# New instruction orders and PSUM banks for a polysketch attention with a gated feed-forward, and batch 1's loads held by a small copy

## The chip, the core and the metric

The kernel runs on one core of one Trainium2 chip. A core has five engines with instruction queues of their own: PE (TensorE, matrix products into PSUM), DVE (VectorE), ACT (ScalarE), POOL (GpSimd) and SP (SyncE, which issues DMA transfers). They run side by side and meet only at semaphores. PSUM has eight banks. The metric is the device time of one execution in microseconds (us); less is better. The median of three runs before the change is 101.96 us.

## The reference

```python
def phi(x):                       # S1, S2: 8 x 32; x: [4 batches, 4 heads, 1088, 32]
    a = np.einsum('rd,bhsd->bhsr', S1, x)
    b = np.einsum('rd,bhsd->bhsr', S2, x)
    return np.einsum('bhsi,bhsj->bhsij', a, b).reshape(*x.shape[:-1], r * r)
q_p, k_p = (phi(q), phi(k))
kv = np.einsum('bhsf,bhsd->bhfd', k_p, v)
z = np.sum(k_p, axis=2)
num = np.einsum('bhsf,bhfd->bhsd', q_p, kv)
den = np.einsum('bhsf,bhf->bhs', q_p, z)[..., None] + 1e-06
attn = num / den
x = attn.transpose(0, 2, 1, 3).reshape(4352, 128)
gate = np.maximum(x @ w_gate, 0.0)        # w_gate, w_val: 128 x 1536
val = x @ w_val
out = gate * val @ w_out                  # w_out: 1536 x 128, out: 4352 x 128
```

This is linear attention with 64 features for each row, and then a feed-forward with a rectified gate over the 4352 rows that it gives.

## The kernel before

The program is written as a list of 857 operations (`P.add(engine, name, function, after, ...)`), each for one engine. A table of numbers, `START`, gives each operation its place; operations are issued in the order of these numbers, so every engine's queue is a part of that one order, and each engine works through its queue in order. `after` and `RINGS` name predecessors for the search that made the table; at run time only true conflicts over data make an engine wait. A second table, `BANKS`, gives each piece of PSUM that is taken (a `Lease`) its bank or pair of banks, and a bank that is taken again waits for the reader that gives it up. Batch 0's first half has a path of its own (`class First`), for an early start; the other queries go through `class Q`, the keys of each batch through `class K`, the feed-forward through `class F`.

- Keys of a batch: load k, two DVE transposes to kT (`kt1`), PE products with the sketches (`ksk`), a DVE transpose back to kab (`kt2`), feature products kp on POOL (`kphi`; some of batch 0 on DVE), then `kv` on PE against v (cast to 16 bits by ACT, `vc`), and `kve` on DVE, which writes bd. The sum z goes PE, DVE (`zc`), PE (`w`), DVE (`wc`) into the query weights wq.
- Queries: load q, DVE transposes to qT (`qt1`), PE products with wq (`qsk`), DVE transposes to qabc (`qt2`), a denominator (`bw`, `red`, `rd`), features qqp on POOL (`qphi`), a transpose on SP's queue or PE (`qtr`), the numerator on PE (`num`), and a copy to xT. In `First` the names are fab, fqp, fpt, frT, and DVE writes xT (`xd`).
- Feed-forward: the rows are cut into groups, and each group into units of 512 columns of gate and value. 102 units each have a gate product `g` and a value product `v` on PE (0.22 us each), `relu` on ACT, a product `h` on DVE out of PSUM (for 19 units ACT copies the value and POOL multiplies, `hp`), and then an output block `o` of four matmuls, accumulated in PSUM over the units of a group. w_gate, w_val and w_out are used in thirds 0, 1, 2. Third 0 comes by SP and is cast by ACT (`cw`); thirds 1 and 2 (wg1, wv1, wg2, wv2, wo1, wo2) are loaded and cast by POOL's own transfers (L310).

Ahead of the named matmuls in `WARM`, PE is given matmuls of zeros into bank 7 (L1015), 55 in all. `gate` (L391) is a memset by POOL of one element of batch 1's k buffer: the load of k for batch 1 overwrites it, and so waits until POOL has come so far; the loads of q and v that follow stand behind it on SP's queue.

Of the kernel before, what the change touches and what calls it, by code (L numbers as in the profile page):

```python
# [10 lines left out]
FP16 = mybir.dt.float16  # L11
# [17 lines left out]
RINGS = [['ld s1', 'ld s2', 'ld k01', 'ld v000', 'ld v001', 'ld v002', 'ld v003', 'ld v010', 'ld v011', 'ld v012', 'ld v013'], ['mz', 'kt1 0 0'], ['fills', 'kt1 0 0'], ['zero', 'fills'], ['ld k00', 'ld q00', 'table'], ['zero', 'mz'], ['zero', 'sel'], ['id32', 'masks', 's1r'], ['kphi 0 8', 'ld wv1', 'ld wg2', 'ld wg1', 'ld wv2', 'gate', 'ld wo1', 'ld wo2'], ['ld v013', 'ld wg0', 'ld wv0', 'ld q01']]  # L29
# [71 lines left out]
]  # L101
WARM = {34: 29, 63: 2, 143: 14, 147: 1, 152: 9}


class Lease:
# [36 lines left out]
def kernel(  # L142
# [12 lines left out]
    nc = tc.nc  # L155
# [26 lines left out]
    def sb(shape, dt, name):  # L182
        return const.tile(shape, dt, name=name)

    P = Plan()
# [867 lines left out]
```

## Time and profile before

| | us |
|---|---|
| runs | 101.83, 101.96, 102.0 |
| span of the profiled execution | 100.1 |
| median of the runs less that span | 1.9 |
| PE busy | 94.2 |
| DVE busy | 82.7 |
| ACT busy | 84.1 |
| POOL busy | 65.8 |
| first feed-forward matmul starts | 14.58 |
| last matmul ends | 96.6 |

The execution's own time beyond its span is not listed, so the span is set beside the median of the runs. Rows of a timeline read: start, duration, engine, line of the kernel, operation, output and inputs, sizes, count, and in brackets how long the engine had been idle and what ended that. A matmul's duration includes its way through the array, so consecutive ones overlap. Rows of the chain read: start, duration, what the program's end hung on then. Buffers of one name are numbered in the program and unnumbered in the profile.

### The profile page before, as it was taken

Reading aid. Unit: us, or ns where it says so; the run is one execution under the profiler, and the core shown is the slowest. Engines: PE = TensorE matmul, PEld = TensorE weight load, DVE = VectorE, ACT = ScalarE, POOL = GpSimd, SP = SyncE. Lnnn points to the kernel's source line nnn. Section 1 sums busy time; section 2 is a strip of 40 time slices with the busy share of each in tenths; the row PEclk is TensorE's granted clock in tenths of the full one; section 3 lists DMA queues with packets and bytes.
Section 4 is the critical chain, followed back from the end, with each engine's and each line's share of the span. In section 5 each row is a group of like instructions: output and inputs, shape, how many; then the busy total and the mean of one; then the engine's idle time right before and its main releaser. Section 6 shows DMA issues by size and latency. Waiting matters only on the chain.

```text
span 100.1 us, 3180 instructions
## 1 busy us (share of the span) xinstructions
PE 94.2 (94%) x1223; PEld 68.3 (68%) x1223; DVE 82.7 (83%) x175; ACT 84.1 (84%) x169; POOL 65.8 (66%) x89
## 2 busy tenths in 40 slices
PE   6999989989999999999999999999999999999950
PEld 6978969848779965557673656765676665688940
DVE  4778779999989998999998689799746879897940
ACT  3445889999799798998999999899999999998730
POOL 6029947898988999999897699935944404001700
PEclk9999999999999999999999999999999999999999
DMA  2988889999930525208664200071217305003331
GB/s 43 370 229 267 146 122 358 339 269 276 342 125 0 111 66 134 45 12 235 165 182 99 60 0 7 1 169 27 52 29 120 78 0 129 2 7 84 99 105 52
DMA packets 14799, 12.40 MB, mean 124 GB/s; under 512 B 8256, under 2 KB 12352, under 8 KB 14784
## 3 DMA queue, kind: packets, MB, share of 16 engines
q1 hardware_dynamic: 13392, 10.70, 38.5%
q0 software_dynamic: 864, 0.79, 5.8%
q10 hardware_dynamic: 528, 0.72, 2.2%
q8 instruction: 9, 0.15, 0.7%
q14 instruction: 6, 0.05, 0.2%
HBM read 9.05 MB, written 2.23 MB: 113 GB/s over the span
## 4 chain that ended last, share of the span: by engine, by line
PE 81%; ACT 6%; POOL 4%; DMA 3%; issue 1%; DVE 1%
PE ps L916 42%; PE ps L944 23%; PE ps L1015 5%; ACT g_sb L921 4%; DMA wg<-in_moe_w_gate_dram 3%; PE ps L848 3%; PE ps L501 2%; PE ps L780 2%; POOL kp L543 2%; PE ps L567 2%; ACT v_sb L925 1%; POOL fqp L695 1%; ACT qpt L840 1%; PE ps L515 1%; POOL wv L310 1%
## 5 line engine op out<-in xcount | busy, mean ns | idle before, releaser
L921 ACT ACTIVATE g_sb<-ps 128x512 f16<-128x512 f32 x102 | 56.3, 613 | 3.9 <-PE ps L916 3.2
L931 DVE TENSOR_TENSOR ht<-g_sb,ps 128x512 f16<-128x512 f16 (+1 forms) x84 | 53.5, 673 | 7.2 <-PE ps L916 5.6
L916 PE MATMUL ps<-xT,wv 128*128 128x512 f16 (+1 forms) x132 | 35.6, 332 | 0.5 <-ACT g_sb L921 0.5
L916 PE MATMUL ps<-xT,wg 128*128 128x512 f16 (+1 forms) x132 | 34.3, 332 | 0.3 <-DMA wg<-in_moe_w_gate_dram 0.3
L944 PEld LDWEIGHTS <-ht 128*128 128x128 f16 x408 | 28.0, 98 | 9.2 <-issue 0.8
L944 PE MATMUL ps<-wo,ht 128*128 128x128 f16 x408 | 33.8, 219 | 0.0
L936 POOL TENSOR_TENSOR ht<-g_sb,v_sb 128x512 f16<-128x512 f16 x19 | 21.7, 1158 | 16.4 <-ACT g_sb L921 14.9
L916 PEld LDWEIGHTS <-wg 128*128 128x128 f16 x132 | 13.6, 115 | 5.9 <-issue 2.2
L543 POOL TENSOR_TENSOR kp<-kab 128x512 f16<-128x512 f32 (+2 forms) x14 | 15.7, 1136 | 2.0 <-DVE kab L507 2.0
L916 PEld LDWEIGHTS <-wv 128*128 128x128 f16 x132 | 13.9, 114 | 3.6 <-issue 1.3
L821 POOL TENSOR_TENSOR qqp<-qan,qabc 128x1024 f16<-128x1024 f32 (+1 forms) x9 | 14.9, 1658 | 0.4
L925 ACT CAST v_sb<-ps 128x512 f16<-128x512 f32 x19 | 11.3, 601 | 0.6 <-PE ps L916 0.5
L1015 PE MATMUL ps<-zero 128*128 128x128 f16 x55 | 5.9, 285 | 1.0 <-DVE zero L292 1.0
L793 DVE STREAM_TRANSPOSE qabc<-ps 128x128 f32<-128x128 f32 (+1 forms) x12 | 5.4, 488 | 1.0 <-PE ps L780 0.6
L987 DVE STREAM_TRANSPOSE qT<-q_sb 128x544 f32<-128x544 f32 (+2 forms) x9 | 5.9, 662 | 0.4 <-DMA q_sb<-in_q_dram 0.4
L1015 PEld LDWEIGHTS <-zero 128*128 128x128 f16 x55 | 5.1, 136 | 1.3 <-DVE zero L292 1.0
L951 ACT ACTIVATE o_sb<-ps 128x512 f32<-128x512 f32 (+1 forms) x10 | 5.2, 521 | 0.7 <-PE ps L944 0.7
L801 POOL TENSOR_TENSOR bw<-qabc 128x128 f32<-128x128 f32 (+1 forms) x9 | 3.7, 412 | 2.9 <-DVE qabc L793 2.9
L815 POOL TENSOR_TENSOR qan<-qabc,qrd 128x128 f32<-128x128 f32 (+1 forms) x9 | 3.3, 372 | 3.3 <-DVE qrd L811 3.3
L861 ACT CAST xT<-ps 128x512 f16<-128x512 f32 (+1 forms) x9 | 4.7, 517 | 0.5 <-PE ps L848 0.5
L491 DVE STREAM_TRANSPOSE kT<-k_sb 128x544 f32<-128x544 f32 x6 | 4.2, 724 | 0.0
L507 DVE STREAM_TRANSPOSE kab<-ps 128x576 f32<-128x576 f32 (+2 forms) x5 | 3.3, 664 | 0.7 <-PE ps L501 0.7
(94 smaller groups left out, 77.4 us busy)
## 6 DMA issues: line engine op xcount, KB each, us to landing
k_sb<-in_k_dram SPq DMA_DIRECT2D x3, 544.0 KB, 6.1
q_sb<-in_q_dram SPq DMA_DIRECT2D x3, 544.0 KB, 4.9
out_dram<-o_sb SPq DMA_DIRECT2D x22, 64.0 KB, 1.7
v<-in_v_dram SPq DMA_DIRECT2D x6, 144.0 KB, 7.7
v<-in_v_dram SPq DMA_DIRECT2D x6, 128.0 KB, 7.6
out_dram<-o_sb SPq DMA_DIRECT2D x16, 32.0 KB, 1.8
v<-in_v_dram SPq DMA_DIRECT2D x6, 64.0 KB, 3.1
k_sb<-in_k_dram SPq DMA_DIRECT2D x1, 288.0 KB, 3.5
```

The lines of the kernel that those rows point to most:

```text
L543: eng.tensor_tensor(out=self.kp[:, lo:hi].rearrange("p x g (i a c) -> p (x g i) a c", i=2, a=R), in0=a[:, :, :, None].to_broadcast([128, n ...
L793: nc.vector.transpose(self.abc[:, lo:lo + m, 2 * i2:2 * i2 + 2].rearrange("p x h f -> p h x f"), pair(ls[i2])[:, :, lo * 32:(lo + m) * 32] ...
L821: nc.gpsimd.tensor_tensor(out=self.qp[:, lo:hi].rearrange("p x g (i a c) -> p (x g i) a c", i=2, a=R), in0=self.an[:, lo * H:hi * H, :, No ...
L916: nc.tensor.matmul(bank(l)[:, y * self.W:(y + 1) * self.W], w[:, j // 4, :, j % 4], x, start=True, stop=True, skip_group_check=True)
L921: nc.scalar.activation(out=self.gs, in_=bank(l), func=ACTF.Relu)
L925: nc.scalar.copy(out=self.vs, in_=bank(l))
L931: nc.vector.tensor_tensor(out=self.ht[:, t], in0=self.gs[:, t], in1=bank(l)[:, t], op=ALU.mult)
L936: nc.gpsimd.tensor_tensor(out=self.ht, in0=self.gs, in1=self.vs, op=ALU.mult)
L944: nc.tensor.matmul(o[:, s], self.ht[:, i * 128:(i + 1) * 128], wo[:, j // 4, j % 4], start=(j == 0 and s == 0), stop=(j == NJ - 1), skip_g ...
L951: nc.scalar.mul(out=self.os[:, 0:n * DM], in_=bank(self.lo)[:, 0:n * DM], mul=1.0 / (XSCALE * XSCALE))
L987: nc.vector.transpose(qT[b][:, lo:hi], q_sb[b][:, lo:hi])
L1015: nc.tensor.matmul(PS[:, 7, 0:128], zero, zero, start=True, stop=True, skip_group_check=True)
```

## The change

Four things change. All of `START` and all of `BANKS` are replaced (each pair of banks is now one of neighbours, as it mostly was). In `RINGS` POOL's loads of weights have the order wg1, wv1, wg2, wv2, wo1, wo2, and no longer stand behind a key product. `WARM` loses 13 of the 55 zero matmuls. And `gate` is now a DMA that SP issues: it copies 16 bytes of the landed third 2 of w_gate into a new buffer, so that SP waits until that third has landed, and with SP everything behind it on its queue.

```diff
-RINGS = [..., ['kphi 0 8', 'ld wv1', 'ld wg2', 'ld wg1', 'ld wv2', 'gate', 'ld wo1', 'ld wo2'], ['ld v013', 'ld wg0', 'ld wv0', 'ld q01']]
+RINGS = [..., ['ld wg1', 'ld wv1', 'ld wg2', 'ld wv2', 'ld wo1', 'ld wo2'], ['ld v013', 'ld wg0', 'ld wv0', 'ld q01']]
 START = [
-    2, 5, 0, 8, 4, 42, 10, 11, 12, 16, 18, 23, 25, 29, 3, 13, 1, 14, 33, 68, 36, 87, 20, 98, 71,
+    2, 6, 1, 8, 5, 40, 9, 10, 12, 13, 15, 23, 26, 29, 3, 17, 0, 19, 33, 80, 37, 93, 20, 58, 65, 79,
...
 BANKS = [
-    (0,), (2,), (3, 4), (5, 6), (1,), (5,), (3,), (7,), (6, 7), (5,), (2,), (6,), (5, 6), (6,),
+    (0,), (0,), (1,2), (6,7), (3,), (1,), (7,), (6,), (3,4), (3,), (7,), (5,), (1,2), (7,), (6,),
...
-WARM = {34: 29, 63: 2, 143: 14, 147: 1, 152: 9}
+WARM = {34: 29, 143: 13}
...
-    g_op = P.add("POOL", "gate", lambda: nc.gpsimd.memset(k_sb[1][0:1, 0:1], 0.0))
+    gone = sb([1, 8], FP16, "gone")
+    g_op = P.add("SP", "gate", lambda: nc.sync.dma_start(
+        out=gone, in_=wg[0:1, 2, 0:2].rearrange("m p j -> m (p j)")), [lwl["g2"][1]])
```

Line numbers after the change are 3 to 5 less: L916 becomes L913, L310 becomes L305, L491 becomes L488.

On POOL, at the end of the start-up (s1r, feature products of batch 0's keys into kp and queries into fqp, weight loads by `DMA`), the queue before is:

```order
L379 TENSOR_TENSOR s1r<-wq,maskh 128x128
L543 TENSOR_TENSOR kp_93<-kab_91 128x512
L543 TENSOR_TENSOR kp_93<-kab_91 128x256
L310 DMA wv<-in_moe_w_val_dram 128x512
L695 TENSOR_TENSOR fqp<-fab 128x512
L310 DMA wg<-in_moe_w_gate_dram 128x512 x2
L695 TENSOR_TENSOR fqp<-fab 128x512
L310 DMA wv<-in_moe_w_val_dram 128x512
L391 MEMSET k_sb_75 1x1
L801 TENSOR_TENSOR bw<-qabc_111 128x8x8
L310 DMA wo<-in_moe_w_out_dram 128x512 x2
```

and after the change:

```order
L374 TENSOR_TENSOR s1r<-wq,maskh 128x128
L692 TENSOR_TENSOR fqp<-fab 128x512
L540 TENSOR_TENSOR kp_93<-kab_91 128x512
L692 TENSOR_TENSOR fqp<-fab 128x512
L305 DMA wg<-in_moe_w_gate_dram 128x512
L540 TENSOR_TENSOR kp_93<-kab_91 128x256
L305 DMA wv<-in_moe_w_val_dram 128x512
L305 DMA wg<-in_moe_w_gate_dram 128x512
L305 DMA wv<-in_moe_w_val_dram 128x512
L305 DMA wo<-in_moe_w_out_dram 128x512 x2
L798 TENSOR_TENSOR bw<-qabc_111 128x8x8 x2
```

Both query products moved ahead of all weight loads, the loads now stand together (thirds 1, 1, 2, 2 of gate and value, then the output weights), the memset is gone, and batch 0's denominators (`bw`) come after all of them.

On DVE, from batch 0's last start-up steps to the transposes of batch 1's keys (kT_86 from k_sb_75), the queue before is:

```order
L626 COPY frx<-frd 128x256
L987 STREAM_TRANSPOSE qT_87<-q_sb_76 128x576
L573 TENSOR_TENSOR bd<-ps,maskg 128x128
L715 TENSOR_TENSOR xT<-ps,frT 128x256
L793 STREAM_TRANSPOSE qabc_111<-ps 128x2x2x32 x4
L807 TENSOR_REDUCE qdn_129<-bw 128x8
L811 RECIPROCAL qrd_133<-qdn_129 128x8
L715 TENSOR_TENSOR xT<-ps,frT 128x256
L931 TENSOR_TENSOR ht<-g_sb,ps 128x512
```

and after the change:

```order
L623 COPY frx<-frd 128x256
L570 TENSOR_TENSOR bd<-ps,maskg 128x128
L984 STREAM_TRANSPOSE qT_87<-q_sb_76 128x576
L712 TENSOR_TENSOR xT<-ps,frT 128x256
L790 STREAM_TRANSPOSE qabc_111<-ps 128x2x2x32 x3
L712 TENSOR_TENSOR xT<-ps,frT 128x256
L804 TENSOR_REDUCE qdn_130<-bw 128x8
L790 STREAM_TRANSPOSE qabc_111<-ps 128x2x2x32
L808 RECIPROCAL qrd_134<-qdn_130 128x8
L928 TENSOR_TENSOR ht<-g_sb,ps 128x512 x2
```

bd moved ahead of the transpose of q's second half, and the second half of xT ahead of the first denominator.

On SP, from batch 0's last load on (q_sb_76), before:

```order
L270 DMA q_sb_76<-in_q_dram 128x576
L394 DMA k_sb_75<-in_k_dram 128x1088
L400 DMA q_sb_77<-in_q_dram 128x1088
L394 DMA k_sb_74<-in_k_dram 128x1088
L264 DMA v_0_79<-in_v_dram 32x4x288
L264 DMA v_1_80<-in_v_dram 32x4x288 x2
L264 DMA v_0_79<-in_v_dram 32x4x256
L264 DMA v_1_80<-in_v_dram 32x4x256 x2
```

and after the change:

```order
L265 DMA q_sb_76<-in_q_dram 128x576
L387 DMA gone<-wg 1x8x1
L391 DMA k_sb_75<-in_k_dram 128x1088
L397 DMA q_sb_77<-in_q_dram 128x1088
L391 DMA k_sb_74<-in_k_dram 128x1088
L259 DMA v_0_79<-in_v_dram 32x4x288
L397 DMA q_sb_78<-in_q_dram 128x1088
L259 DMA v_0_79<-in_v_dram 32x4x256
L259 DMA v_1_80<-in_v_dram 32x4x288 x2
L259 DMA v_1_80<-in_v_dram 32x4x256 x2
```

The copy that waits for the weight stands ahead of all loads of batches 1 and 2 (k_sb_75, q_sb_77, v_1_80 are batch 1's; k_sb_74, q_sb_78, v_0_79 batch 2's), and batch 2's q and a piece of its v now come ahead of batch 1's v.

More of the change, by code (lines that the diff above doesn't have):

```diff
@@ L28 @@
 FILL = 'DVE'
-RINGS = [['ld s1', 'ld s2', 'ld k01', 'ld v000', 'ld v001', 'ld v002', 'ld v003', 'ld v010', 'ld v011', 'ld v012', 'ld v013'], ['mz', 'kt1 0 0'], ['fills', 'kt1 0 0'], ['zero', 'fills'], ['ld k00', 'ld q00', 'table'], ['zero', 'mz'], ['zero', 'sel'], ['id32', 'masks', 's1r'], ['kphi 0 8', 'ld wv1', 'ld wg2', 'ld wg1', 'ld wv2', 'gate', 'ld wo1', 'ld wo2'], ['ld v013', 'ld wg0', 'ld wv0', 'ld q01']]
+RINGS = [['ld s1', 'ld s2', 'ld k01', 'ld v000', 'ld v001', 'ld v002', 'ld v003', 'ld v010', 'ld v011', 'ld v012', 'ld v013'], ['mz', 'kt1 0 0'], ['fills', 'kt1 0 0'], ['zero', 'fills'], ['ld k00', 'ld q00', 'table'], ['zero', 'mz'], ['zero', 'sel'], ['id32', 'masks', 's1r'], ['ld wg1', 'ld wv1', 'ld wg2', 'ld wv2', 'ld wo1', 'ld wo2'], ['ld v013', 'ld wg0', 'ld wv0', 'ld q01']]
 Q0E = 'ACT'
```

123 rows, old and new, of tables (BANKS, START) are left out of this document.

## Prediction, made before the changed kernel ran

> **What bounds the kernel now.** I read the page first, then the windows by stage, then the chain, then the timelines of each engine over the first 40 us.
>
> ```profile
> span 100.1 us, 3180 instructions
> ...
> PE 81%; ACT 6%; POOL 4%; DMA 3%; issue 1%; DVE 1%
> ```
> ```profile
> 14.58:21.28 6.70, 6.06 (x50) 5.03 (x51) 6.62 (x18) 6.44 (x14) 5.37 (x9) 1.00 1.02 312
> 21.28:41.00 19.72, 19.34 (x331) 14.84 (x330) 18.36 (x37) 17.32 (x37) 18.48 (x19) 1.00 0.58 156
> ...
> 60.00:97.00 37.00, 36.58 (x376) 25.59 (x374) 30.29 (x52) 33.76 (x66) 16.56 (x17) 1.00 0.26 58
> ```
>
> The chain is PE for 81%. The window rows (length, then busy PE, PEld, DVE, ACT, POOL) show three regimes. From 60 us on PE alone is full, so that part takes as long as its matmuls, and the change removes none of those. From 14.58 to 21.28, DVE (6.62 of 6.70) and ACT are the full ones. From 21 to 41, DVE and POOL are within 1.4 us of PE. Time can thus be won or lost in two ways: by when the first expert unit starts, and by which of DVE, POOL and PE gives way before 50 us.
>
> ```profile
> 9.65 1.08 POOL fqp L695
> 10.73 0.52 POOL wg L310
> 11.26 3.28 DMA wg<-in_moe_w_gate_dram
> ...
> 30.69 0.66 PE ps L916 x6
> 31.34 0.89 PE ps L944 x16
> ```
> ```profile
> 13.74 0.50 PE L780 MATMUL ps<-qT,wq 32*32 32x128 f32 x32
> 14.58 0.63 PE L916 MATMUL ps<-xT,wg 128*128 128x256 f16 x4 [0.34 <-DMA wg<-in_moe_w_gate_dram]
> ...
> 21.28 0.71 PE L501 MATMUL ps<-kT,wS 64*32 64x288 f32 x16
> ...
> 26.20 0.73 PE L780 MATMUL ps<-qT,wq 32*32 32x256 f32 x32
> ```
>
> The chain into the first unit (14.58) is POOL's queue and then the landing of the second gate third, the last of POOL's first three weight loads.
>
> **Part 1: the start.** The first unit is now one of third 0, whose weights ACT casts, so it no longer waits for a POOL load. It still needs xT, which takes bd, the ACT copies and q's transpose.
>
> ```profile
> 12.51 0.78 DVE L987 STREAM_TRANSPOSE qT<-q_sb 128x576 f32<-128x576 f32 x1 [0.41 <-DMA q_sb<-in_q_dram]
> 13.21 0.25 DVE L573 TENSOR_TENSOR bd<-ps,maskg 128x128 f16<-128x128 f32 x1
> 13.93 0.42 DVE L715 TENSOR_TENSOR xT<-ps,frT 128x256 f16<-128x256 f32 x1 [0.47 <-PE ps L708]
> 14.43 0.91 DVE L793 STREAM_TRANSPOSE qabc<-ps 128x128 f32<-128x128 f32 x4
> ```
> ```profile
> 7.31 1.66 POOL L543 TENSOR_TENSOR kp<-kab 128x512 f16<-128x512 f32 x2 [1.53 <-DVE kab L507]
> ...
> 10.67 1.13 POOL L310 DMA_DIRECT2D wg<-in_moe_w_gate_dram  x2
> ```
> ```profile
> 12.38 0.59 ACT L641 COPY fpt<-ps 128x512 f16<-128x512 f16 x1
> 12.86 0.62 ACT L316 CAST wv<-qabc 128x512 f16<-128x512 f32 x1
> ```
> ```profile
> 4.75 1.44 PE L1015 MATMUL ps<-zero 128*128 128x128 f16 x14
> ```
>
> bd stood behind a transpose that waited for q until 12.51; now it stands ahead. POOL now runs fqp, kp, fqp before any weight: from fab (about 6.7, its transpose now right behind k's) 1.08 + 1.07 + 1.08, with kab at 7.9, ends at 10.1. The gate third is issued by 10.65, the last kp piece (0.63) done by 11.3, the last kv matmul at 11.5, bd at 12.15. ACT, with its 0.4 to 0.6 us copies in the new order, frees the bank of the first numerator at about 12.45 (the second fpt copy now stands ahead of wv's cast), PE has the numerator at 12.8, q's transpose ends at 13.25, xT's first half is written from 13.2 to 13.6, and batch 0's query matmuls (0.50) run on PE from 13.35. First unit: 13.9 in place of 14.58, a gain of 0.7. Bounds: 0.35 (only the 0.34 wait goes) and 1.0 (q lands 0.3 earlier, since no POOL load competes before 10 us). The 13 zero matmuls left out cost nothing either way: 12 of them filled waits of PE, and one (1.44 for 14: 0.10) stood ahead of the first query matmul.
>
> **Part 2: the gate.** After wg1 POOL issues wv1 (11.3 to 12.0), wg2 (12.5), wv2, wo1, wo2 (to 14.2).
>
> ```profile
> wv<-in_moe_w_val_dram POOLq DMA_DIRECT2D x2, 128.0 KB, 4.0
> wg<-in_moe_w_gate_dram POOLq DMA_DIRECT2D x2, 128.0 KB, 3.2
> ```
> ```profile
> L394 SPq DMA_DIRECT2D k_sb<-in_k_dram x3: 327/346/376, 13.7 to 22.8; - x3
> ...
> DMA to landing us min/median/max: 5.2/6.1/7.0
> ```
> ```profile
> q1 hardware_dynamic: 153, 0.61, 66.5%
> ```
> ```profile
> 17.66 1.83 DVE L931 TENSOR_TENSOR ht<-g_sb,ps 128x512 f16<-128x512 f16 x3
> 19.41 1.36 DVE L491 STREAM_TRANSPOSE kT<-k_sb 128x544 f32<-128x544 f32 x2
> ```
>
> wg2 starts to be issued at 12.0 and lands 3.2 (the gate loads' median) later: 15.2. Then SP issues its copy (about 0.4) and k of batch 1 at 15.7, where before it was 13.7. Behind SP's wait stand all loads of batch 1 and 2; the earlier ones are out by 7.7. The landing of this k was not recorded. Its cost has these ends: at most 5.7 (issued 13.7, read without a wait at 19.41), and at least 3.3: in the window 14.6 to 17.0 SP's queue, q1, counts 153 packets, and k's 128 come first. I take 4.0, nearer the packets, as recorded loads of this size (5.2 to 7.0) had others ahead or beside them. So k lands at 19.7 (19.0 to 21.4).
>
> When does DVE want it? What it does between the first xT half and the first product is the same set; it begins with batch 0's query results at 14.05 in place of 14.43, so it is 0.35 ahead. But it now has six products (0.6 each) ahead of k's transposes instead of five: 19.41 - 0.35 + 0.6 = 19.7. So the gate costs DVE 0 to 1.7, and I take 0.1. PE's key matmuls of batch 1 (21.28 before) need both transposes, done at about 21.2.
>
> **Part 3: the order behind it.** Up to batch 1's query matmuls (26.20 in the row above) PE's new order holds 32 gate and value units and 6 output blocks since the first unit, against 30 and 4 before: 4 x 0.22 = 0.88 us more work done. (In the chain 6 half-width matmuls, three units, take 0.66, and 16 output matmuls, four blocks, 0.89: 0.22 for each.) These matmuls need wc of batch 1, which DVE reaches after the same instructions as before, at about 26.1 (25.97 before, less the 0.25 to 0.35 lead of Part 2, plus the waits for k and for PE's later key matmuls). So PE is at the same place at the same time and 0.88 ahead in work.
>
> ```profile
> 25.97 0.17 DVE L532 COPY wq<-ps 128x32 f32<-128x32 f32 x1
> ...
> 27.29 1.29 DVE L793 STREAM_TRANSPOSE qabc<-ps 128x512 f32<-128x512 f32 x2
> ```
>
> Not all of it stays. Ahead of gate unit 15 PE has 18 units and blocks, query, key and four small matmuls, 18 x 0.22 + 0.73 + 0.6 + 0.12 = 5.4; its bank comes free with product 21, before which DVE has three products (1.83), two transposes of k and q (1.36), two of query results (1.29), one of key results (0.7, as k's) and three small ones (0.55): 5.75. So DVE takes 0.35 back: what is late next is DVE, and PE can't be more than about 0.55 ahead. POOL, the next in line, has the same instructions in another order; its heavy stretch ends with batch 2's last kp, which I count at 49.3 against PE's wish of 49.4, so it takes nothing, but has nothing to spare. From 55 us on DVE and POOL have slack, and the 0.55 stays to the end. The rest of the reorder I cost at nothing: PE is gapless there before, and its work is the same.
>
> **The sum.** The chain gives 0.88 - 0.35 = 0.55 (rounded) off the span of 100.1: 99.55. The median of the three runs shown is 101.96, 1.9 above the span; with that kept, 101.4.
>
> **The skill beside it.** The Trainium skill, "DMA: Bandwidth & Descriptors", section "Anatomy of one DMA — SWDGE (gpsimd) path", gives about 2.0 us and bytes at 436 GB/s for a load issued by POOL. That would be 2.3 us for 128 KB; the 3.2 and 4.0 of the rows disagree, as they were taken with a loaded SP queue. By the page wg2 lands at 14.3, k at 18.8, DVE never waits, and the sum would be 0.1 better: 101.3.
>
> **Rivals.**
> (a) The gate opens late and the loss is larger than the gain. Place: DVE before k's transposes. Every us that k lands after 19.7 holds DVE (full in the window rows), and behind it PE. It decides at 20.3, where the 0.55 is used up. With a k load of 5.2 (the shortest recorded) it lands at 20.9, 1.2 late: 101.4 + 1.1 = 102.5. For it: a value third took 4.0, not 3.2. Against: once q is in, nothing competes with POOL's loads until the gate opens. Chance 0.2.
> (b) DVE and POOL are the bound from 14 to 50, and the early start is given back in them: 101.9. For it: 18.36 and 18.48 of 19.72. Against: DVE too begins 0.35 earlier. Chance 0.15.
> (c) The gate helps more: the last POOL loads (wo1, wo2) are out 2 us sooner and units never wait; PE keeps all 0.88, and of the 0.64 that PE idles between 14.58 and 21.28 (6.70 less 6.06) a third goes as well: 100.9. Chance 0.2.
> (d) PE's clock. The granted clock is 1.00 in every window, yet the 14 zero matmuls at 4.75 took 0.10 each, and output matmuls of the same shape later 0.89 for 16, 0.056: PE got faster in between, under steady work. If it fell back before 14 us for want of the zero matmuls, the first 15 units (0.22 each) would take 3.3 more, of which ACT's pace hides half: 103. Against: PE's waits there stay under 1 us by my walk. Chance 0.03. The Trainium skill, "TensorE: Matmul & The Clock Gate", Part 1, has PE fall back to half rate after an idle window of about 3.4 us; by that rule (d) would be nil, and no run here shows one yet.
>
> **How the numbers follow.** Likeliest, at 0.42: 101.4, own range 101.1 to 101.75. Adding (c) below and most of (a) above gives 100.8 to 102.5, with about 0.1 left out on each side. A measurement of this kernel tells about 0.2% (0.2 us) from no change. Faster takes the likeliest and (c), a little of it lying within 0.2: 0.61; the same takes (b) and the edges: 0.17; slower (a) and (d): 0.22.
>
> **What would show it.** In the new profile: the first L913 matmul at about 13.9 with no wait for wg; bd ahead of qT on DVE; POOL's loads one after another until 14.2; k of batch 1 issued at about 15.7; the two kT transposes beginning at 19.7, with a wait for k_sb of under 0.5; the 32x256 query matmuls at about 26.2; from 60 us on the same rows, 0.55 earlier. I am wrong if DVE shows a wait of 0.6 or more for k_sb, if PE shows a wait for wv near 14.5 that starves ACT, or if waits of PE for DVE or POOL between 27 and 50 add up to more than 0.9.

## Result, and the profile after

The changed kernel is slower: 105.7 us in the median of 4 runs (104.79 to 106.49) against 101.97 for the kernel before (101.83 to 102.0) on the same chip, a ratio of 1.034 (95% interval 1.027 to 1.041). Run again later, beside some of the experiments, it was 104.16 us against 102.29, a ratio of 1.018 (1.014 to 1.021). So it loses 1.8 to 3.4%, some 2 to 4 us, where 0.55 us of gain was forecast. Executions of one kernel scatter by 1 to 6%, so a time below is the median of all runs, while a ratio takes only those within 1.5% of their kernel's fastest (5 of 11 for the copy of an earlier third, 4 of 9 where only two edits are mended). A profile shows one execution, which may be longer than its kernel's median.

The profiled execution took 104.79 us. Its page, with span and chain:

```profile
span 103.0 us, 3144 instructions
...
PE 39%; POOL 20%; DMA 16%; ACT 9%; DVE 5%; issue 3%; SPq 3%; ACTq 1%; DVEq 0%; POOLq 0%
```

Before, PE was 81% of the chain. Now it is 39%, and POOL and DMA, 7% before, have 36%, with 3% of SP's queue: the end hangs on deliveries, that is on loads and on what POOL hands over. The three windows of the prediction, in the changed kernel (length, busy PE, PEld, DVE, ACT, POOL, clock, DMA share, GB/s):

```profile
14.58:21.28 6.70, 5.87 (x60) 5.29 (x58) 5.07 (x14) 6.48 (x14) 4.44 (x8) 1.00 0.94 196
21.28:41.00 19.72, 17.97 (x308) 13.01 (x307) 17.85 (x35) 15.56 (x34) 16.41 (x16) 1.00 0.78 191
60.00:97.00 37.00, 36.64 (x356) 24.73 (x354) 29.78 (x52) 33.93 (x68) 18.20 (x18) 1.00 0.23 51
```

In the middle window every engine is less busy than before (PE 17.97 against 19.34, POOL 16.41 against 18.48): none became the bound, all waited more. DVE in the first window fell from 6.62 to 5.07. After 60 us little changed. The clock is 1.00 in all three.

PE's timeline at the three places that the prediction named and at its wait for wv, of the changed kernel:

```profile
14.11 0.82 PE L913 MATMUL ps<-xT,wg 128*128 128x256 f16 x6
15.39 0.63 PE L913 MATMUL ps<-xT,wv 128*128 128x256 f16 x4 [0.46 <-DMA wv<-in_moe_w_val_dram]
...
22.36 1.24 PE L498 MATMUL ps<-kT,wS 64*32 64x288 f32 x16 [0.68 <-DVE kT L488]
...
28.05 0.73 PE L777 MATMUL ps<-qT,wq 32*32 32x256 f32 x32
```

The first unit starts 0.47 us earlier (14.58 before). Batch 1's query matmuls start 1.85 later (26.20 before); less the 0.88 of work that the new order has done by then, PE is 0.97 behind. The chain (its pieces up to DVE's transpose of batch 3's q) says why:

```profile
12.24 3.77 DMA wg<-in_moe_w_gate_dram
...
16.02 0.78 SPq L387
16.84 4.59 DMA k_sb<-in_k_dram
21.46 0.76 DVE kT L488
...
39.49 1.95 POOL qqp L818
...
43.84 5.53 DMA q_sb<-in_q_dram
49.40 0.75 DVE qT L984
```

wg2 lands, SP issues its copy, then k of batch 1, and DVE takes k the moment that it is there. In the timelines of DVE and ACT the waits stand in brackets:

```profile
21.46 1.37 DVE L488 STREAM_TRANSPOSE kT<-k_sb 128x544 f32<-128x544 f32 x2 [1.63 <-DMA k_sb<-in_k_dram]
...
25.25 0.75 DVE L488 STREAM_TRANSPOSE kT<-k_sb 128x544 f32<-128x544 f32 x1 [0.53 <-DMA k_sb<-in_k_dram]
```
```profile
30.81 0.67 ACT L554 CAST v<-v 128x576 f16<-128x576 f32 x1 [1.96 <-DMA v<-in_v_dram]
```

DVE was ready for k at 21.46 - 1.63 = 19.83, and then waits for batch 2's k as well. ACT was ready to cast batch 1's v at 28.85. Its row in the kernel before:

```profile
30.76 1.25 ACT L557 CAST v<-v 128x576 f16<-128x576 f32 x2
```

There it came to v 1.9 us later and did not wait. The new order wants v sooner and loads it behind batch 2's q. PE waits in its turn behind these (its timeline):

```profile
33.08 0.88 PE L913 MATMUL ps<-xT,wg 128*128 128x256 f16 x4 [0.38 <-ACT v_sb L922]
...
50.77 0.38 PE L913 MATMUL ps<-xT,wv 128*128 128x512 f16 x1 [0.85 <-DVE ht L928]
```

The second is DVE's wait for batch 3's q (49.40 in the chain). With two waits of 0.17 and 0.19 after 70 us these make 1.6, and with the 0.97 by 28.05 us 2.6 of the 2.9 by which the span grew.

In the chain batch 3's q hangs on POOL. POOL's timeline in the changed kernel, and then in the kernel before, around the query features `qqp` of batch 1's second half:

```profile
35.88 1.15 POOL L933 TENSOR_TENSOR ht<-g_sb,v_sb 128x512 f16<-128x512 f16 x1
37.84 1.15 POOL L933 TENSOR_TENSOR ht<-g_sb,v_sb 128x512 f16<-128x512 f16 x1 [0.81 <-ACT v_sb L922]
39.00 0.41 POOL L812 TENSOR_TENSOR qan<-qabc,qrd 128x128 f32<-128x128 f32 x1
39.49 1.95 POOL L818 TENSOR_TENSOR qqp<-qan,qabc 128x1024 f16<-128x1024 f32 x1
```
```profile
35.28 1.96 POOL L821 TENSOR_TENSOR qqp<-qan,qabc 128x1024 f16<-128x1024 f32 x1
37.19 3.39 POOL L936 TENSOR_TENSOR ht<-g_sb,v_sb 128x512 f16<-128x512 f16 x3
```

Two gating products (units 14 and 15) now stand ahead of these features, so they are done at 41.44 instead of 37.24. The transpose of them is next on SP's queue and batch 3's q behind it, issued at 43.84.

That is not later than in the kernel before, though, as SP's and DVE's timelines of that kernel show:

```profile
44.40 0.42 SPq L400 DMA_DIRECT2D q_sb<-in_q_dram  x1
```
```profile
49.45 0.73 DVE L987 STREAM_TRANSPOSE qT<-q_sb 128x544 f32<-128x544 f32 x1
```

There q was issued at 44.40, and DVE took it at 49.45 without a wait. In the changed kernel DVE comes to it at 49.40 - 1.11 = 48.29, 1.2 sooner, and the load takes 5.5 us against 4.1. So the wait for q comes from DVE being there sooner and from the longer load, not from a later issue.

### The profile page after: what moved, and what is told of

Its sections match the earlier page's. It is cut to its first block, busy times and chain, and to the rows that moved or that the text cites. A ratio compares the mean times of both kernels' runs of the same rounds, so it can differ in the third digit from the quotient of the medians.

```text
span 103.0 us, 3144 instructions
## 1 busy us (share of the span) xinstructions
PE 94.6 (92%) x1210; PEld 68.3 (66%) x1210; DVE 81.9 (80%) x175; ACT 82.7 (80%) x169; POOL 65.6 (64%) x88
## 4 chain that ended last, share of the span: by engine, by line
PE 39%; POOL 20%; DMA 16%; ACT 9%; DVE 5%; issue 3%; SPq 3%; ACTq 1%; DVEq 0%; POOLq 0%
PE ps L913 18%; PE ps L941 11%; POOL ht L933 7%; DMA q_sb<-in_q_dram 5%; ACT g_sb L918 5%; PE ps L1012 5%; DMA k_sb<-in_k_dram 4%; POOL kp L540 4%; POOL qqp L818 4%; DMA wg<-in_moe_w_gate_dram 4%; DMA qpt<-qqp 3%; DVE ht L928 2%; ACT v_sb L922 2%; POOL fqp L692 2%; PE ps L498 2%
## 5 line engine op out<-in xcount | busy, mean ns | idle before, releaser
L918 ACT ACTIVATE g_sb<-ps 128x512 f16<-128x512 f32 x102 | 55.4, 622 | 5.9 <-PE ps L913 4.3
L913 PE MATMUL ps<-xT,wv 128*128 128x256 f16 (+1 forms) x132 | 34.5, 332 | 1.9 <-DVE ht L928 0.8
L941 PEld LDWEIGHTS <-ht 128*128 128x128 f16 x408 | 27.5, 98 | 11.3 <-issue 2.4
L913 PE MATMUL ps<-xT,wg 128*128 128x512 f16 (+1 forms) x132 | 34.2, 331 | 0.6 <-ACT v_sb L922 0.4
L941 PE MATMUL ps<-wo,ht 128*128 128x128 f16 x408 | 33.3, 219 | 0.0
L913 PEld LDWEIGHTS <-wv 128*128 128x128 f16 x132 | 13.9, 114 | 4.7 <-issue 1.5
L913 PEld LDWEIGHTS <-wg 128*128 128x128 f16 x132 | 13.8, 113 | 4.7 <-issue 1.2
L818 POOL TENSOR_TENSOR qqp<-qan,qabc 128x1024 f16<-128x1024 f32 (+1 forms) x9 | 14.9, 1657 | 0.6
L488 DVE STREAM_TRANSPOSE kT<-k_sb 128x544 f32<-128x544 f32 x6 | 4.3, 730 | 2.2 <-DMA k_sb<-in_k_dram 2.2
L1012 PE MATMUL ps<-zero 128*128 128x128 f16 x42 | 4.8, 313 | 1.0 <-DVE zero L287 1.0
L554 ACT CAST v<-v 128x576 f16<-128x576 f32 x6 | 4.1, 678 | 2.0 <-DMA v<-in_v_dram 2.0
L1012 PEld LDWEIGHTS <-zero 128*128 128x128 f16 x42 | 4.3, 147 | 1.0 <-DVE zero L287 1.0
L498 PE MATMUL ps<-kT,wS 64*32 64x288 f32 (+2 forms) x80 | 3.7, 372 | 0.7 <-DVE kT L488 0.7
```

The costliest lines, as they stand in the source:

```text
L498: nc.tensor.matmul(bank(la, p)[32 * a:32 * a + 32, lo * 32:hi * 32], wt, self.kT[rows, c * 32:(c + m) * 32], start=True, stop=True, skip_g ...
L818: nc.gpsimd.tensor_tensor(out=self.qp[:, lo:hi].rearrange("p x g (i a c) -> p (x g i) a c", i=2, a=R), in0=self.an[:, lo * H:hi * H, :, No ...
L913: nc.tensor.matmul(bank(l)[:, y * self.W:(y + 1) * self.W], w[:, j // 4, :, j % 4], x, start=True, stop=True, skip_group_check=True)
L918: nc.scalar.activation(out=self.gs, in_=bank(l), func=ACTF.Relu)
L941: nc.tensor.matmul(o[:, s], self.ht[:, i * 128:(i + 1) * 128], wo[:, j // 4, j % 4], start=(j == 0 and s == 0), stop=(j == NJ - 1), skip_g ...
L1012: nc.tensor.matmul(PS[:, 7, 0:128], zero, zero, start=True, stop=True, skip_group_check=True)
```

## Experiments

Moves are written as new places in `START`, which sets the order of every queue. The numbers on the left are operations: 40 the gate, 49 to 51 the pieces v21, v22 and v23 of batch 2's v, 52 and 58 the q of batches 2 and 3, 213 to 217 the second half of batch 1's queries (denominator sum and reciprocal on DVE, L812 and L818 on POOL, the transpose on SP), 26 and 29 the loads wo1 and wo2. Each line added or taken away ahead of an operation shifts its line number, mostly by 2. All ratios are to the kernel before, run beside it.

The first theory was that the late gate is the main cause (G); its rivals were the new order itself, with SP's list of loads first (O, later L for the loads and P for POOL's list), and the zero matmuls that are gone (W). What stood at the end is that several of these late chains run side by side (S).

### The gate and the zero matmuls, one at a time

**The old gate in the changed kernel.**

```diff
-    gone = sb([1, 8], FP16, "gone")
-    g_op = P.add("SP", "gate", lambda: nc.sync.dma_start(
-        out=gone, in_=wg[0:1, 2, 0:2].rearrange("m p j -> m (p j)")), [lwl["g2"][1]])
+    g_op = P.add("POOL", "gate", lambda: nc.gpsimd.memset(k_sb[1][0:1, 0:1], 0.0))
+for i, s in {40: 90.5}.items():
+    START[i] = s
```

> The changed kernel with the old gate alone: the SyncE copy is replaced by the POOL memset of one element of k_sb, which stands right behind the issue of wv2 (about 13.3 us); everything else, the new order and banks included, stays. Theory G (the late gate is the main cause: k of batch 1 issued at 16.84 cost DVE 1.63 us at 19.83, and all loads behind it, k2, v1 and q3, come late with it): k1 is issued at about 13.4, 3.4 us sooner, lands before 19, DVE's waits for k (1.63 and 0.53) and ACT's wait of 2.0 for v of batch 1 go, the 32x256 query matmuls return from 28.05 to about 26.3, and the time falls from 105.7 to 101.3 to 102.3. Theory O (the new order costs most by itself, since SyncE now loads batch 2's q and one of its v pieces ahead of batch 1's v, and q3 late): only the 1 us lost by 28 us returns, 103.3 to 104.5, with the waits for v near 30 us and for q3 near 49 us still there. Theory W (PE's zero matmuls that were left out): no change, 105 to 106.

105.18 us, 1.030 (1.022 to 1.039): hardly any gain. (The number lies in W's range; the zero matmuls put back, below, answer that.) The timelines of DVE and ACT in its profiled execution, the longest of the four at 107.18 us:

```profile
20.50 1.37 DVE L488 STREAM_TRANSPOSE kT<-k_sb 128x544 f32<-128x544 f32 x2 [0.62 <-DMA k_sb<-in_k_dram]
```
```profile
31.90 0.67 ACT L554 CAST v<-v 128x576 f16<-128x576 f32 x1 [3.61 <-DMA v<-in_v_dram]
```

k was issued 3.3 us sooner (13.55) and was there only 1 us sooner: it took 6.9 us, beside POOL's weight loads. And ACT's cast of v was no sooner (31.90 against 30.81). With hardly any gain in time, theory G alone falls.

**The copy of an earlier third.**

```diff
-        out=gone, in_=wg[0:1, 2, 0:2].rearrange("m p j -> m (p j)")), [lwl["g2"][1]])
+        out=gone, in_=wg[0:1, 1, 0:2].rearrange("m p j -> m (p j)")), [lwl["g1"][1]])
```

> The changed kernel with its SyncE copy reading the first POOL third of w_gate (landed at 13.47) instead of the second (16.00): the gate keeps its kind and opens 2.5 us sooner. Theory G: k1 is issued at about 14.3 instead of 16.84, lands at 18.5 to 19.5, DVE waits under 0.2 for it, and the time is 101.5 to 102.5, at most 0.5 from the kernel with the old gate. Theory O: 103.3 to 104.5. If the SyncE copy costs by its kind and not by its time (it holds the queue and the copy's own 0.78 us), it stays 1 us or more behind the kernel with the old gate.

103.92 us (102.23 to 106.25), 1.010 (1.004 to 1.015): better than with the old gate on the same chip, and by the ratio between the ranges of G and O. So it isn't the copy's kind that costs. That this gate, which opens a little later than the old one, does better than it is measured; why is not shown.

**The new gate in the kernel before.**

```diff
-    g_op = P.add("POOL", "gate", lambda: nc.gpsimd.memset(k_sb[1][0:1, 0:1], 0.0))
+    gone = sb([1, 8], FP16, "gone")
+    g_op = P.add("SP", "gate", lambda: nc.sync.dma_start(
+        out=gone, in_=wg[0:1, 2, 0:2].rearrange("m p j -> m (p j)")), [lwl["g2"][1]])
+for i, s in {40: 95.5}.items():
+    START[i] = s
```

> The kernel before with the new gate alone: the POOL memset is replaced by the SyncE copy of the second third of w_gate, which landed at 13.88 there; order and banks of before. k1 is then issued at about 14.7 instead of 13.7. Theory G (cost goes by the time at which k lands against DVE's wish at 19.4): k1 lands at 18.7 to 19.7, cost 0 to 0.5, 101.9 to 102.5. If the copy costs by its kind: 103 or more. Theory O: 101.9 to 102.2 as well, since the order is the old one; this run tells the kind of the gate from its time, not G from O.

103.08 us (101.97 to 104.9), 1.005 (1.000 to 1.011): by the ratio 0.5 us, the upper end of what was expected. Where it costs, in its DVE and PE timelines:

```profile
25.68 0.74 DVE L495 STREAM_TRANSPOSE kT<-k_sb 128x544 f32<-128x544 f32 x1 [1.38 <-DMA k_sb<-in_k_dram]
```
```profile
27.75 0.73 PE L784 MATMUL ps<-qT,wq 32*32 32x256 f32 x32 [1.43 <-DVE wq L536]
```

Batch 1's k is in time there (a wait of 0.15); the next load, batch 2's k, is not. Here the late gate is paid at the load behind it that has the least to spare.

**The zero matmuls put back.**

```diff
-WARM = {34: 29, 143: 13}
+WARM = {34: 29, 63: 2, 143: 14, 147: 1, 152: 9}
```

> The changed kernel with the table of zero matmuls of before (12 more at three places between 8 and 14 us). Theory W (PE runs slower for want of them): 102 to 103.5. Theories G and O: no change, 104.8 to 106.2, and a first expert unit at about 14.1 to 14.3.

104.76 us, 1.024 (1.014 to 1.034), between the two results of the changed kernel: nothing to be told. Its profiled execution has a lesson of its own (page, PE's timeline):

```profile
span 101.8 us, 3170 instructions
...
PEclk9999859999999999999999999999999999999998
```
```profile
16.13 0.84 PE L913 MATMUL ps<-xT,wg 128*128 128x256 f16 x6
...
28.20 0.73 PE L777 MATMUL ps<-qT,wq 32*32 32x256 f32 x32
```

The granted clock fell there for two slices, with the zero matmuls in place, and the first unit began 2 us later than in the changed kernel. By the query matmuls the difference was 0.15, and this execution ended 1.2 us sooner. In these two executions the start did not set the time.

### SP's list of loads

**Batch 1's v first.**

```diff
+for i, s in {52: 178.3, 49: 178.6}.items():
+    START[i] = s
```

> The changed kernel (1.034 times the kernel before) with one move in SyncE's list: the loads of batch 2's q (557 KB) and of its piece v21 are issued behind batch 1's four v pieces instead of ahead of them. Theory L (what costs is when each load lands against the place that the new order gives its reader; ACT casts batch 1's v at 28.85 now, at 30.76 before, and v landed at 30.7): v of batch 1 lands about 2 us sooner, near 28.7, ACT's wait of 2.0 falls under 0.5, PE's two stalls of 0.54 and 0.28 behind it go, and the ratio falls to 1.018 to 1.028. Theory G (the late k alone): no change, 1.03 or more. If all of what is lost stands behind v, below 1.015.

105.59 us, 1.026 (1.020 to 1.031): the number lies in L's range, but also between the two results of the changed kernel, so nothing is told.

**Batch 3's q early.**

```diff
+for i, s in {58: 222.5}.items():
+    START[i] = s
```

> The changed kernel with one move in SyncE's list: batch 3's q is loaded right behind v22, at about 28.5 us, instead of at 43.84 behind two transposes and five stores that wait for POOL and DVE. Theory L: q lands near 34, DVE's wait of 1.1 at 49.4 and PE's stall of 1.0 behind it go, ratio 1.022 to 1.028; the load's 557 KB delay v31 and the first stores, which nothing waits for. Theory G: the wait at 49.4 only passes the late start on, and its place is taken by another: 1.03 or more.

104.82 us, 1.019 (1.013 to 1.024), below L's range and near the lower result of the changed kernel: no gain that can be told.

**Both, and the gate on the earlier third.**

```diff
-        out=gone, in_=wg[0:1, 2, 0:2].rearrange("m p j -> m (p j)")), [lwl["g2"][1]])
+        out=gone, in_=wg[0:1, 1, 0:2].rearrange("m p j -> m (p j)")), [lwl["g1"][1]])
+for i, s in {52: 178.3, 49: 178.6, 58: 222.5}.items():
+    START[i] = s
```

> The changed kernel with three edits: the SyncE copy reads the first POOL third of w_gate (gate some 2.5 us sooner), batch 1's v ahead of batch 2's q and v21, and batch 3's q behind v22. Theory L: the three waits (k and k2, v, q3) go or fall by most, 1.6 + 0.5 of DVE's, 0.8 and 1.0 of PE's: 0.995 to 1.008. If something else in the new order sets the time (POOL's and DVE's lists), it stays above 1.012.

104.14 us, 1.022 (1.016 to 1.028). I expected about 1.00. The waits that I had aimed at are gone or smaller (DVE still waits 0.54 and 0.65 for k), and two others stand in their place (ACT's and PE's timelines):

```profile
34.84 0.67 ACT L556 CAST v<-v 128x576 f16<-128x576 f32 x1 [1.58 <-DMA v<-in_v_dram]
```
```profile
46.46 0.41 PE L847 MATMUL ps<-qpt,bd 128*64 128x512 f16 x2 [1.41 <-DMA qpt<-qqp]
```

The first is batch 2's v, the second the transpose of POOL's late half. In the profile of the changed kernel PE came to that place at 45.03, too late to wait.

**POOL's last weight loads later, with the old gate.**

```diff
+    g_op = P.add("POOL", "gate", lambda: nc.gpsimd.memset(k_sb[1][0:1, 0:1], 0.0))
+for i, s in {40: 90.5, 26: 107.5, 29: 121.5}.items():
+    START[i] = s
```

> The changed kernel with the old POOL gate behind wv2 and, as in the kernel before, POOL's loads wo1 and wo2 put back behind the two bw products, so that they are issued at about 15 to 17 us instead of 13.5 to 14.6, right beside k1. In the run with the old gate alone (ratio 1.030) k1 was issued at 13.55 and landed only at about 20.45, against at most 19.41 before. Theory C (POOL's loads beside k1, q1 and k2 slow these): k1 lands at 18.5 to 19.5, k2 2 us sooner than 24.66, ratio 1.010 to 1.020. If they are slow by themselves or by SyncE's list: 1.025 to 1.035.

106.85 us, 1.043 (1.037 to 1.050), worse. k was issued at 13.37 and read at 19.50 without a wait, so it took at most 6.1 us, against 6.9 with wo1 and wo2 beside it. But the new order wants wo1 early. From the list of its waits (us in total, times, longest):

```profile
PE ps L941 <- DMA wo<-in_moe_w_out_dram: 3.0, 1, 3.0
```

### POOL's list

**The late half moved ahead of one of the two products.**

```diff
+for i, s in {213: 290.2, 214: 290.4, 215: 300.6, 216: 300.8, 217: 309.5}.items():
+    START[i] = s
```

> Theory P, formed from the traces of the runs so far: in the new order POOL makes the second half of batch 1's query features (L812 and L818, 2.4 us) behind two gating products (L933) instead of ahead of them, done at 41.4 instead of 37.2; the DMA transpose of it then lands at 44.5 to 48.6 (41.2 before), PE wants it at about 44.9, and batch 3's q stands behind that transpose on SyncE. In the six runs with the new order in which PE got there in time it stalled 1.1 to 1.6 us at that place. This kernel is the changed one with that piece and the two DVE instructions that it needs put ahead of the second of these products, and its transpose one place earlier on SyncE. P: the features are done near 39.6, the transpose lands by 43.5, q3 is issued near 42 and the wait of 1.1 for it at 49.4 goes: ratio 1.015 to 1.026 against 1.03 for the changed kernel. If that half is late only because everything is: no change, 1.03 or more.

105.14 us, 1.018 (1.013 to 1.023). By the number alone P's range is met, but against the changed kernel beside it (next) nothing is gained. In its profiled execution waits for v (2.8 on ACT), k (1.8 on DVE) and batch 1's q (1.7 on DVE) stand, and the features were done at 41.89, no sooner than without the move. DVE did not wait for batch 3's q there.

**The changed kernel again**, without an edit.

> The changed kernel as it is, on the chip of these three runs, so that they are compared with it under the same conditions: 1.024 to 1.036.

104.16 us, 1.018 (1.014 to 1.021), below what was expected.

**The same part alone, in the kernel before**: its features put behind the two products.

```diff
+for i, s in {215: 323.3, 216: 323.6, 217: 323.8}.items():
+    START[i] = s
```

> The kernel before with only the POOL order of the new one at this place: the second half of batch 1's query features (done at 37.2) stands behind the two gating products that followed it, and its transpose keeps its place. P: done near 39.5, transpose landed at 42.9 to 44, PE, which wants it at 42.4, stalls 0.5 to 1.6: ratio 1.005 to 1.016. If the place is not what costs: 0.998 to 1.003.

103.83 us (103.38 to 104.68), 1.018 (1.013 to 1.022), above what was expected (1.005 to 1.016): in the old order this one move costs as much as the whole change on that chip. POOL's and PE's timelines:

```profile
36.80 2.28 POOL L938 TENSOR_TENSOR ht<-g_sb,v_sb 128x512 f16<-128x512 f16 x2 [1.88 <-ACT v_sb L927]
...
39.52 1.96 POOL L823 TENSOR_TENSOR qqp<-qan,qabc 128x1024 f16<-128x1024 f32 x1
```
```profile
42.64 0.40 PE L946 MATMUL ps<-wo,ht 128*128 128x128 f16 x4 [1.15 <-POOL ht L938]
...
44.27 0.41 PE L850 MATMUL ps<-qpt,bd 128*64 128x512 f16 x2 [0.38 <-DMA qpt<-qqp]
```

The products wait for ACT's copies, and POOL stands idle for 1.88 (in the changed kernel 0.81). Everything after is late: the features, whose transpose PE waits for, and unit 17's product behind them, for which it waits longer.

### All lists mended, and each part put back

**All at once**: the gate on the earlier third, batch 1's v first, all of batch 2's v ahead of the first store, batch 3's q ahead of the transposes, POOL's half early.

```diff
-        out=gone, in_=wg[0:1, 2, 0:2].rearrange("m p j -> m (p j)")), [lwl["g2"][1]])
+        out=gone, in_=wg[0:1, 1, 0:2].rearrange("m p j -> m (p j)")), [lwl["g1"][1]])
+for i, s in {52: 178.3, 49: 178.6, 51: 206.3, 50: 206.6, 58: 222.5, 213: 290.2, 214: 290.4, 215: 300.6, 216: 300.8, 217: 309.5}.items():
+    START[i] = s
```

> The changed kernel with all lists mended at once: gate on the first POOL third of w_gate, batch 1's v ahead of batch 2's q, all of batch 2's v ahead of batch 3's k and the first store, batch 3's q right behind, and POOL's second half of batch 1's query features early as in the run beside it. Theories L and P together: no wait of DVE over 0.7 for k, none of ACT for v over 0.5, no stall of PE over 0.7 behind 20 us; the early start of 0.5 us stays: ratio 0.990 to 1.004. If a further list (DVE's products, the PSUM banks) sets the time: above 1.010.

102.77 us (101.59 to 103.92, 12 runs), 1.000 (0.997 to 1.004): the loss is gone. The page, DVE's and POOL's timelines of its profiled execution, the fastest of the 12:

```profile
span 99.8 us, 3143 instructions
```
```profile
20.41 1.37 DVE L490 STREAM_TRANSPOSE kT<-k_sb 128x544 f32<-128x544 f32 x2 [0.80 <-DMA k_sb<-in_k_dram]
```
```profile
35.98 1.96 POOL L820 TENSOR_TENSOR qqp<-qan,qabc 128x1024 f16<-128x1024 f32 x1
```

The first unit starts at 14.02 here, 0.56 before the old one, and the ratio is 1.000: the early start earns nothing that the ratio shows. Which wait takes it, these runs do not settle. The new banks, the new orders of PE and ACT, and DVE's but for two instructions are still in this kernel, so no loss of theirs can be told.

**Each part put back alone** into this kernel. First the gate of the change:

```diff
-        out=gone, in_=wg[0:1, 1, 0:2].rearrange("m p j -> m (p j)")), [lwl["g1"][1]])
+        out=gone, in_=wg[0:1, 2, 0:2].rearrange("m p j -> m (p j)")), [lwl["g2"][1]])
```

> The kernel with all lists mended (1.000 times the kernel before), but with the gate of the change, the SyncE copy of the second third of w_gate: k1 issued near 16.5 instead of 14.2. Theory S (several chains of about the same length end between 20 and 50 us: the gate's k, batch 1's v, POOL's second half with its transpose, batch 3's q; the start is given away as soon as one of them is late, and mending some leaves the time at the next): k lands near 21, DVE waits 1.3 to 1.8 for it and k2 0.5, ratio 1.008 to 1.018. If the late gate is nothing: 0.998 to 1.003.

103.83 us, 1.014 (1.006 to 1.021). DVE's timeline:

```profile
21.26 1.37 DVE L490 STREAM_TRANSPOSE kT<-k_sb 128x544 f32<-128x544 f32 x2 [1.52 <-DMA k_sb<-in_k_dram]
...
24.36 0.74 DVE L986 STREAM_TRANSPOSE qT<-q_sb 128x544 f32<-128x544 f32 x1 [1.16 <-DMA q_sb<-in_q_dram]
...
26.60 0.74 DVE L490 STREAM_TRANSPOSE kT<-k_sb 128x544 f32<-128x544 f32 x1 [0.83 <-DMA k_sb<-in_k_dram]
```

DVE waits for both k and, between them, for batch 1's q, which stands behind the gate too. Next, the queries' second half at its place in the change:

```diff
-for i, s in {52: 178.3, 49: 178.6, 51: 206.3, 50: 206.6, 58: 222.5, 213: 290.2, 214: 290.4, 215: 300.6, 216: 300.8, 217: 309.5}.items():
+for i, s in {52: 178.3, 49: 178.6, 51: 206.3, 50: 206.6, 58: 222.5}.items():
```

> The kernel with all lists mended, but with POOL's order of the change: the second half of batch 1's query features behind both gating products. Theory S: its transpose lands at 46.2 to 46.6, PE, there at about 43 to 44.8, stalls 1.3 to 2: ratio 1.012 to 1.020, about what the run with the three edits without it showed. If the place is nothing: 0.998 to 1.003.

103.69 us, 1.010 (1.006 to 1.015). Its profiled execution, 104.52, had k late as well, and the expected stall at the transpose was only 0.34 in it: the time, a little below the range, speaks for the theory; the trace does not show it there.

Batch 2's q ahead of batch 1's v:

```diff
-for i, s in {52: 178.3, 49: 178.6, 51: 206.3, 50: 206.6, 58: 222.5, 213: 290.2, 214: 290.4, 215: 300.6, 216: 300.8, 217: 309.5}.items():
+for i, s in {51: 206.3, 50: 206.6, 58: 222.5, 213: 290.2, 214: 290.4, 215: 300.6, 216: 300.8, 217: 309.5}.items():
```

> The kernel with all lists mended, but with batch 2's q and v21 ahead of batch 1's v on SyncE as in the change. Theory S: batch 1's v lands near 28 to 28.5 instead of 26 to 26.5, ACT, which casts it at 27.4, waits about 1, ratio 1.003 to 1.010. If the order of these loads is nothing: 0.998 to 1.003.

102.88 us, 1.002 (0.997 to 1.007): not told from nothing, although ACT waited 2.6 for v in the profiled execution.

Batch 2's last v pieces and batch 3's q late:

```diff
-for i, s in {52: 178.3, 49: 178.6, 51: 206.3, 50: 206.6, 58: 222.5, 213: 290.2, 214: 290.4, 215: 300.6, 216: 300.8, 217: 309.5}.items():
+for i, s in {52: 178.3, 49: 178.6, 213: 290.2, 214: 290.4, 215: 300.6, 216: 300.8, 217: 309.5}.items():
```

> The kernel with all lists mended, but with batch 2's last v pieces behind the first store and batch 3's k, and batch 3's q behind both transposes, as in the change: q3 issued near 42, landed at 46.5 to 47.5, wanted by DVE at 46.0. Theory S: DVE waits 0.5 to 1.5 for q3, and ACT up to 1 for batch 2's v: ratio 1.004 to 1.012. If nothing: 0.998 to 1.003.

103.14 us, 1.003 (0.998 to 1.008): not told from nothing.

**Only the two that cost by themselves mended** in the changed kernel:

```diff
-        out=gone, in_=wg[0:1, 2, 0:2].rearrange("m p j -> m (p j)")), [lwl["g2"][1]])
+        out=gone, in_=wg[0:1, 1, 0:2].rearrange("m p j -> m (p j)")), [lwl["g1"][1]])
+for i, s in {213: 290.2, 214: 290.4, 215: 300.6, 216: 300.8, 217: 309.5}.items():
+    START[i] = s
```

> The changed kernel with only the two edits that cost by themselves when put back: the gate on the first third and POOL's second half early; SyncE's order of v, q2 and q3 stays that of the change. Theory S with these two as the cause: 1.000 to 1.008. If the order of SyncE's loads carries as much: 1.010 to 1.018.

103.9 us, 1.007 (1.004 to 1.010). Alone in the changed kernel, POOL's half gained nothing (1.018) and the gate some (1.010); by the ratios the two together bring back most of the loss. This is the weakest of the ratios: the median lies 1.8% above the 102.02 of the kernel before, and 1.007 cannot be told from the 1.010 of the gate alone. The 0.7% that is left would be SP's list, whose two parts were too small to tell one by one.

**The gate opened at once** in the kernel with all mended, to look for a version that beats both.

```diff
+    g_op = P.add("POOL", "gate", lambda: nc.gpsimd.memset(k_sb[1][0:1, 0:1], 0.0))
+for i, s in {40: 79.5, 52: 178.3, 49: 178.6, 51: 206.3, 50: 206.6, 58: 222.5, 213: 290.2, 214: 290.4, 215: 300.6, 216: 300.8, 217: 309.5}.items():
+    START[i] = s
```

> The kernel with all lists mended, with the old kind of gate (a POOL memset) set right behind the issue of wv1, so that k1 is issued at about 12.3 instead of 14.2. Theory S: DVE's waits of 0.8 and up for k go, and of the 0.5 us of earlier start some stays: ratio 0.992 to 1.000, the first version that beats the kernel before. If k1 then slows wg2, wv2 and q of batch 0 instead: 1.000 to 1.010.

104.14 us, 1.018 (1.014 to 1.022), the rival's side and beyond. PE's timeline and the clock row of the page show what the gate guards:

```profile
16.77 1.04 PE L913 MATMUL ps<-xT,wv 128*128 128x256 f16 x4 [2.10 <-DMA wv<-in_moe_w_val_dram]
```
```profile
PEclk9999996699999999999999999999999999999999
```

With k issued at 12.14, wv1 (issued at 11.39) landed at 16.73 instead of 15.12 in the kernel with all mended. Around the end of the wait and behind it, from 15.3 to 20.4, the granted clock was below 0.7 in two slices; how much of the loss is the wait's and how much the clock's is not told apart (the one run at full clock took 103.03). Opened at 12 the gate starves the first units, opened at 16.8 it starves DVE; 14.2 was the best tried. No kernel here beats the one before.

## Why the prediction was wrong

- **Part 1, the start: right.** First unit at 14.11 (13.9 forecast; 0.47 gained against 0.7, inside 0.35 to 1.0), POOL's loads issued one after another until 14.37 (14.2), bd ahead of qT.
- **Part 2, the gate: right in mechanism, mis-sized in four terms that all erred the same way.** wg2 was issued 0.24 later and landed 3.77 after its issue instead of 3.2 (16.00 against 15.2); the copy held the queue until 16.84, 0.84 after the landing instead of 0.5; k took 4.59 instead of 4.0. So k was there at 21.43, not 19.7. DVE wanted it at 19.83, as worked out. The cost to DVE was 1.63 where 0.1 was taken, at the end of the range named (1.7): for k a value near the lower end of its range (3.3 to 5.7) was taken, for wg2 the median of two loads in another order, and for the copy about 0.4, for which no row stood. The reason given against rival (a), that nothing competes with POOL's loads once q is in, left out POOL's loads themselves: wg2 took 3.77, each of POOL's five others being under way in a part of that time. Rival (a) is what happened, with k 0.5 later than its own price assumed. That batch 2's k pays as well (0.53) was not in it.
- **The estimate beside it.** By the estimate from the Trainium skill, "DMA: Bandwidth & Descriptors", section "Anatomy of one DMA — SWDGE (gpsimd) path", wg2 would have landed at 14.3 and DVE never have waited. The trace disagrees: 3.77 us for wg2 (2.3 by the estimate), and in the issue rows of the profile after a median of 4.2 for the value thirds and 5.3 for the output weights, all 128 KB. Nor was a loaded SP queue the reason for the longer times, as the prediction had it: SP issued nothing between 7.64 and 16.02, and its last load, q, was read by DVE at 12.49, while the value thirds, issued at 11.65 and 12.76, took 3.7 and 4.7.

```profile
wg<-in_moe_w_gate_dram POOLq DMA_DIRECT2D x2, 128.0 KB, 3.5
wv<-in_moe_w_val_dram POOLq DMA_DIRECT2D x2, 128.0 KB, 4.2
wo<-in_moe_w_out_dram POOLq DMA_DIRECT2D x2, 128.0 KB, 5.3
```

- **Part 3: the step that failed outright is "the rest of the reorder I cost at nothing".** POOL was counted by its sum at the end of its heavy stretch (49.3 against 49.4; in the trace batch 2's last kp ended at about 51.3), not by the place of each piece. One piece 4 us later in that list costs 1.0% put back alone, and 1.8% by itself in the old order, where the products ahead of it wait longer. The sign of the warning was there, "has nothing to spare", and no price was put to it. SP's list behind the gate (batch 1's v behind batch 2's q, while ACT wants v 1.9 us sooner) was shown in the order and not costed; the difference of two ratios from two chips (1.007 and 1.000) would give it some 0.6%.
- **Rival (b)** had DVE and POOL as the bound by their work. Neither was; POOL was late by its order, with less work done. **Rival (c)** did not come. **Rival (d)**: the clock stayed at 1.00 in the profile above, and the zero matmuls put back made no difference that can be told. In the profiled execution of the changed kernel's repeat the clock fell to about 0.7 for two slices, but around 37 us, behind a wait of PE of 1.97 that came from batch 1's v, and not near the start.
- **The signs named for being wrong**: the first came, a wait for k_sb of 0.6 or more (1.63). The second came in part: PE waited 0.46 for wv at 15.39, and ACT was not starved (6.48 busy of 6.70). The third did not come as named: from 27 to 50 us PE shows a wait of 0.38, for ACT; its wait of 0.85 for DVE ended at 50.77.

Shown by runs: the late gate (1.4% put back alone) and POOL's late half (1.0% put back, 1.8% alone in the old order), and that the loss is not gone while either is in place. Only argued: which of SP's orders carries the rest, how POOL's late half costs PE time in the new order (its time shows it, its trace hardly), and why the old gate in the changed kernel gained nothing while the copy of the earlier third did.

## What to carry to other kernels

Where a new order is searched, go through the queue of each engine and each DMA queue piece by piece: for every piece that moved back ask who takes it and when, since sums of busy time say nothing of that. Where several chains end at about the same time, mending one may show little or nothing; mend all, then put each back alone. A wait in an in-order queue is to be costed at its bad end: the landing, the waiting issue and a load among others each came out longer here than what had been taken for them.

## What was not expected of the hardware

SP's queue in the changed kernel (its timeline):

```profile
16.02 0.78 SPq L387 DMA_DIRECT2D gone<-wg  x1
16.84 0.43 SPq L391 DMA_DIRECT2D k_sb<-in_k_dram  x1
17.32 1.52 SPq L397 DMA_DIRECT2D q_sb<-in_q_dram  x1
```

The copy of 16 bytes took nearly twice as long to issue as k's 544 KB, and of two loads of 544 KB one took 0.43 to issue and the next 1.52, with others under way. The time from issue to use of batch 1's k was 4.6 us when issued at 16.84, with three of POOL's loads under way in that time, and 6.9 when issued at 13.55, with five: issuing 3.3 us sooner brought it 1 us sooner. One load by POOL of 128 KB (wv1) took 5.3 us (11.39 to 16.73) with k's load started 0.75 us after it, and 3.6 us (11.56 to 15.12) in the kernel with all mended, where k's load started 2.6 us after it.
